# Longer planned times for loads and transposes, later first-layer weights, and four output buffers in a planned attention + mixer kernel

## Chip, cores and metric

One core of one Trainium2 chip. The metric is the device time of one execution in microseconds (us). The kernel before takes 647.9 us (median of three runs, 647.58 to 648.09).

## The reference

```python
# q, k, v: (8, 12, 448, 64) float32, tau = 0.1
q_n = q / (norm(q, axis=-1) + 1e-6);  k_n = k / (norm(k, axis=-1) + 1e-6)
attn = softmax(q_n @ k_n^T / tau)                  # per batch and head, 448 x 448
x = (attn @ v) as (8, 448, 768)
# mixer: U (448, 32), V (32, 448), w_ch1 (768, 3072), w_ch2 (3072, 768)
u = x + (x^T @ U @ V)^T
out = u + relu(u @ w_ch1) @ w_ch2
```

## The kernel before

The kernel has no fixed loop order. It first lists every operation with a planned duration, then a small planner runs the list against a model of the engines and sorts all operations by planned start. That order is what each engine's queue gets, and the trace shows the engine keep to it: in the changed kernel a ScalarE `ln` whose input was there at 59.9 us ran at 68.34, behind the `relu`s planned before it. A wrong planned duration therefore costs nothing in itself; it changes **which instruction stands behind which**. Planned times below come from running this planner by itself.

```python
class Plan:
    def run(self): ...          # greedy: an engine takes the first operation that is ready
                    if isinstance(o.lat, tuple):          # a transfer
                        q, work, fixed = o.lat
                        dma[q] = max(dma[q], o.end) + work      # its queue, one after the other
                        o.end = dma[q] + fixed                  # and a fixed time on top
                    else:
                        o.end += o.lat

def load(fn, busy, deps=(), acq=(), rel=()):              # issued by GpSimd
    return plan.add(Op("POOL", 0.8, fn, ..., lat=("in", busy, 2.0)), pool_q)

r_O = ring(2, [128, CH], FP, "O_sb")                      # results on their way out
r_mm = ring(3, [128, 512], FP, "mm", psum)                # PSUM banks for all but scores and attn @ v

# ... stats(b): VectorE squares and sums q and k per head, ScalarE takes ln and exp,
#     VectorE normalises; then xn is transposed (batches 0, 1: TensorE; others: DMA) ...
o = Op("ACT/DVE" if b == 0 else "DVE", dve_t(256 * (a1 - a0), 2), None, ...)      # the square

# ... stage0(b): U and V products (TensorE), u = x + h (VectorE), transposes of u ...

def mlp(b, us, uT, ut):
    for f in range(NC): ...                               # first layer: 24 x 6 matmuls into one mm bank each
    work = [(i, t, half) for i, t in enumerate(tiles) for half in range(2)]
    side = 3 if b == 0 else 1                             # batch 0: three results side by side,
    for w0 in range(0, len(work), side):                  # since w2 is still arriving
        mms = [Slot(r_mm, 1) for _ in range(side)]
        ...                                               # second layer: 24 matmuls per result
        o = plan.add(Op("DVE", ..., nc.vector.tensor_add(O.tile, mm.tile, us[i]), acq=[O], rel=[mm, us[i]]))
        plan.add(Op("SP", 0.1, nc.sync.dma_start(out=..., in_=O.tile...), rel=[O], prio=2, lat=2.5))

hold = load_v(0, 4, 12)                                   # the rest of v of batch 0
for i in range(NW):
    w1_ops.append(load_w1(i, NW, hold[-4:-3]))            # w1 after the fourth-last of these
```

Of the kernel before, what the change touches and what calls it, by code (L numbers as in the profile page):

```python
# [10 lines left out]
FP = mybir.dt.float32  # L11
# [187 lines left out]
def kernel(  # L199
# [25 lines left out]
    inv_tau = 1.0 / float(tau)  # L225
    EPS = 1e-6
    PE_BATCHES = 2

    const = ctx.enter_context(tc.tile_pool(name="const", bufs=1))
    pool = ctx.enter_context(tc.tile_pool(name="pool", bufs=1))  # L230
# [13 lines left out]
    def fixed_ring(tiles):  # L244
# [15 lines left out]
    r_u = ring(8, [128, C], BF, "u_nat")  # L260
    r_uT = ring(1, [128, CC, 512], BF, "uT")

    r_w2 = Ring(1, lambda i: pool.tile([128, H, 4, D], FP, name="v_raw", tag="w2", bufs=1)
                if i == 0 else pool.tile([128, NC, C], BF, name="w2_sb", tag="w2", bufs=1))
    w2, v_raw = Slot(r_w2, 1), Slot(r_w2, 6)
    r_relu = ring(1, [128, NC, 512], BF, "relu")
    r_O = ring(2, [128, CH], FP, "O_sb")
    r_rd = ring(2, [128, 4, 1], FP, "rd")
    r_mm = ring(3, [128, 512], FP, "mm", psum)
    r_sc = ring(3, [128, 512], FP, "sc", psum)  # L270
    r_av = ring(2, [128, 4, D + 8], FP, "av", psum)


    U_f = const.tile([128, 2, 4, R], FP, name="U_f")
    U_sb = const.tile([128, 2, 4, 128], BF, name="U_sb")
    V_f = const.tile([R, S], FP, name="V_f")
    V_sb = const.tile([128, PAD + S + PAD], BF, name="V_sb")
    ident = const.tile([128, 128], BF, name="ident")
    w1_sb = const.tile([128, CC, F], BF, name="w1_sb")
# [30 lines left out]
    def dve_t(n, fast=1):  # L310
        return 0.09 + n * 0.00104 / fast

    def load(fn, busy, deps=(), acq=(), rel=()):
        return plan.add(Op("POOL", 0.8, fn, deps=deps, acq=acq, rel=rel,
                           lat=("in", busy, 2.0)), pool_q)

    def fill(fn, n=256, prio=8, eng="DVE", deps=()):
        return plan.add(Op(eng, 0.1 + n * 0.0005, fn, deps=deps, prio=prio))


    def load_w1(i, n, deps):
# [33 lines left out]
    def load_qk(b, h0, h1):  # L355
        ld = Slot(r_ld, 3 * (h1 - h0) // 2)
        ops = [load(lambda i=i, src=src: nc.gpsimd.dma_start(  # L357
            out=ld.tile[:, i, 0:h1 - h0, :],
            in_=src[b, h0:h1].rearrange("h (s c) d -> s h (c d)", c=SC)),
            (h1 - h0) * 0.5, acq=[ld]) for i, src in enumerate((q, k))]  # L360
        return ld, ops

    def load_v(b, h0, h1):


        vb = v_t[b % 2]
        old = [v_set[b % 2]] + [last_av.get((b - 2, h // 2)) for h in range(h0, h1)]
        ops = []
        for hh in range(2):
            hs = slice(h0 + hh, h1, 2)  # L370
            for j in range(4):
                if j < 3:
                    lo, hi, base = 128 * j + 64 * hh, 128 * j + 64 * hh + 128, 0
                else:
                    lo, hi, base = (384, 448, 0) if hh == 0 else (0, 64, 64)
                for n, c, s0, s1 in segments(lo, hi):
                    p0 = base + n - lo
                    src = v[b, hs].rearrange("h (s c) d -> c s h d", c=SC)[c, s0:s1]
                    busy = (s1 - s0) * (h1 - h0) * 0.001
                    if b == 0:  # L380
                        ops.append(plan.add(Op("SP", 0.45, lambda j=j, s0=s0, s1=s1, p0=p0, hs=hs,
                                               src=src: nc.sync.dma_start(
                            out=v_raw.tile[p0:p0 + s1 - s0, hs, j, :], in_=src),
                            acq=[v_raw], lat=("x", busy, 2.0), prio=-2)))
                    else:
                        ops.append(load(lambda j=j, s0=s0, s1=s1, p0=p0, hs=hs, src=src:
                            nc.gpsimd.dma_start(out=vb[p0:p0 + s1 - s0, hs, j, 0:D], in_=src),  # L387
                            busy, deps=old))
        loads = ops
        if b == 0:  # L390
            def cast(p, hs, j):
                return plan.add(Op("POOL", 1.2 if j.stop == 3 else 0.3, lambda: nc.gpsimd.tensor_copy(  # L392
                    out=vb[p, hs, j, 0:D], in_=v_raw.tile[p, hs, j, :]),
                    deps=ops + old, rel=[v_raw]), pool_v)
            ops = [cast(slice(0, 128), slice(h0, h1), slice(0, 3)),
                   cast(slice(0, 64), slice(h0, h1, 2), slice(3, 4)),
                   cast(slice(64, 128), slice(h0 + 1, h1, 2), slice(3, 4))]
        for h in range(h0, h1):
            got[b, h, "v"] = ops
        return loads  # L400
# [43 lines left out]
    def norm(b, p, ld, inv, a, deps, pr):  # L444


        by_pe = b < PE_BATCHES
        xn, qkT = Slot(r_xn, 2 if by_pe else 1), Slot(r_qkT, 7)
        deps = deps + [xn_set[count[0] % len(xn_t)]]
        count[0] += 1  # L450

        def part(i, hh):
            def fn():
                src = ld.tile[:, i, a:a + 2, :].rearrange("p h (c d) -> p h c d", d=D)
                sc = inv.tile[:, i, a:a + 2, :].unsqueeze(3)
                if i == 0:
                    dst = xn.tile[:, 8:12, :].rearrange("p c (h d) -> p h c d", h=2)
                    nc.vector.tensor_mul(dst, src, sc.to_broadcast([SCH, 2, SC, D]))  # L458
                else:
                    dst = xn.tile[:, 4 * hh:4 * hh + 4, 64 * hh:64 * hh + 64]  # L460
                    nc.vector.tensor_mul(dst, src[:, hh], sc[:, hh].to_broadcast([SCH, SC, D]))  # L461
            return plan.add(Op("DVE", dve_t(512 if i == 0 else 256), fn, deps=deps, acq=[xn],
                               rel=[ld, inv] if (i, hh) != (1, 0) else [ld, inv], prio=pr))

        ops = [part(1, 0), part(1, 1), part(0, 0)]
        if not by_pe:
            done = [plan.add(Op("SP", 0.1, lambda: nc.sync.dma_start_transpose(
                out=qkT.tile, in_=xn.tile.rearrange("p b e -> p (b e)")), deps=ops, acq=[qkT],
                rel=[xn], prio=0, lat=("x", 0.05 * 84, 2.0)))]
        else:  # L470
            done = []
            for b0, b1 in ((0, 8), (8, 12)):
                done.append(flip(
                    pe_tp, [(lambda z=z: xn.tile[:, z, :]) for z in range(b0, b1)], SCH,
                    lambda: qkT.tile, (lambda t_, x, b0=b0, b1=b1: (t_[:, b0:b1, :], x)),
                    ops, [qkT], [xn]))
        got[b, p, "qkT"] = (qkT, done)
# [127 lines left out]
    def mlp(b, us, uT, ut):  # L605
# [25 lines left out]
        for w0 in range(0, len(work), side):  # L631
# [11 lines left out]
            for (i, t, half), mm in zip(work[w0:w0 + side], mms):  # L643
# [5 lines left out]
                for bb in (b - par, b - par + 1):  # L649
                    o0 = (bb % 2) * S  # L650
                    lo, hi = max(128 * t, o0), min(128 * (t + 1), o0 + S)
                    if lo >= hi:
                        continue
                    for nn, j, p0, p1 in segments(lo - o0, hi - o0):
                        r0 = nn + o0 - 128 * t
                        O.uses += 1
                        O.left += 1
                        plan.add(Op("SP", 0.1, lambda bb=bb, j=j, p0=p0, p1=p1, r0=r0, O=O, hs=hs:
                            nc.sync.dma_start(out=rows(out[bb], j, p0, p1)[:, hs],
                                              in_=O.tile[r0:r0 + p1 - p0, :]),  # L660
                            deps=[o], rel=[O], prio=2, lat=2.5))

    def copy_op(op, dst, src):
        if op.by == "ACT":
# [19 lines left out]
        nc.vector.memset(U_sb, 0.0)  # L684
        nc.vector.memset(V_sb, 0.0)

    zf = fill(lambda: nc.vector.memset(U_f, 0.0), 256, prio=-4)
    z = fill(zero, 1500, prio=-0.2)

    def load_u(par):  # L690
        off = PAD * par
        ops = []
        for t in range(4):
            lo, hi = max(0, 128 * t - off), min(S, 128 * (t + 1) - off)
            for n, c, s0, s1 in segments(lo, hi):
                r0 = n + off - 128 * t
                ops.append(plan.add(Op("SP", 0.45, lambda t=t, c=c, s0=s0, s1=s1, r0=r0: nc.sync.dma_start(
                    out=U_f[r0:r0 + s1 - s0, par, t, :], in_=rows(moe_U, c, s0, s1)),
                    deps=[zf], prio=-2, lat=2.5)))
        return ops  # L700

    def cast_u(par):
        nc.gpsimd.tensor_copy(out=U_sb[:, par, :, 0:R], in_=U_f[:, par])

    def cast_v():
        nc.gpsimd.tensor_copy(out=V_sb[0:R, PAD:PAD + S].rearrange("r (c s) -> r s c", c=SC),
                              in_=V_f.rearrange("r (s c) -> r s c", c=SC))


    w1_ops, w2_ops = [], []  # L710
# [13 lines left out]
        return stage0(b, X, muls)  # L724

    u0 = load_u(0)
    v0 = plan.add(Op("SP", 0.45, lambda: nc.sync.dma_start(out=V_f, in_=moe_V), prio=-2, lat=2.5))
    first = load_qk(0, 0, 2)
    id_set = plan.add(Op("POOL", 0.5, lambda: make_identity(nc, ident)), pool_q)
    stats(0, 0, 2, *first)  # L730
# [4 lines left out]
    hold = load_v(0, 4, 12)  # L735
    u1 = load_u(1)
    for i in range(NW):
        w1_ops.append(load_w1(i, NW, hold[-4:-3]))
    consts = [plan.add(Op("POOL", 0.5, lambda: cast_u(0), deps=u0 + [z]), pool_v),
              plan.add(Op("POOL", 1.5, cast_v, deps=[v0, z]), pool_v),  # L740
              plan.add(Op("POOL", 0.5, lambda: cast_u(1), deps=u1 + [z]), pool_v)]
    state[0] = att(0)
    go(1, 0, 4)
    go(1, 4, 8)
# [52 lines left out]
```

## Time and profile before

| | kernel before |
|---|---|
| span of the profiled run | 647.6 us |
| TensorE work at full rate (worked out in the prediction) | 578.6 us |
| lost: span less that work | 69.0 us |
| of it up to 72 us / 72 to 105 / 105 to 137 | 34.0 / 3.8 / 8.3 |
| 137 to 170 / 170 to 260 / behind 260 | 9.4 / 6.5 / 7.2 |
| VectorE busy from 120 to 220 us | 89.6 of 100 us |

"Lost" is the wall time of a stretch less the full-rate time of the matmuls in it: waits, and running at half clock. It is the measure used all through this text. Read it by stretch, since the busy share of TensorE (93%) mixes a start that is full of waits with 390 us that have almost none. The stretches here differ a little from those in the prediction. Where a trace lacks matmul records, the table's sum is up to 2 us too high, and a single line of it is good to about half a microsecond; span less 578.6 is then the right total.

### The profile page before, as it was taken

The page shows a single profiled execution, that of the slowest core. Times are in us where ns is not written, and L with a number is a line of the kernel's source. Part 1 is how long each engine was busy: PE and PEld are TensorE (multiplying, and loading weights), DVE is VectorE, ACT ScalarE, POOL GpSimd, SP SyncE. Part 2 cuts the span into 40 slices and gives each one's busy share as a digit, 9 for nine tenths or more (in the row PEclk, how much of TensorE's full clock was granted, in tenths as well). Part 3 has the DMA queues.
Part 4 walks back from the last instruction along what each step waited for, and adds up shares of the span by engine and source line. Part 5 has one row for each costly group of instructions (what it writes and reads, how often), then busy time and mean ns, then how long its engine had stood idle before and what let it go on. Part 6 is the DMA issues. An engine that isn't in the chain of part 4 may idle for free.

```text
span 647.6 us, 11512 instructions
## 1 busy us (share of the span) xinstructions
PE 603.9 (93%) x4682; PEld 354.6 (55%) x4682; DVE 303.5 (47%) x736; ACT 286.3 (44%) x605; POOL 114.3 (18%) x175
## 2 busy tenths in 40 slices
PE   2879999696999889999999999999999999999997
PEld 1455665363654457566644566566644666654464
DVE  7946978797999856852670124103410120010011
ACT  5853882485685108650864108640744004204400
POOL 3164533161343400700150000000000000000000
PEclk9987999799899999999999999999999999999999
DMA  9979998999699915924590314212000310210011
GB/s 128 172 134 160 180 204 64 157 131 169 62 159 133 174 45 87 182 30 88 99 134 0 59 53 82 30 25 74 15 13 0 74 50 12 62 55 7 0 50 49
DMA packets 150180, 55.09 MB, mean 85 GB/s; under 512 B 115280, under 2 KB 150128, under 8 KB 150128
## 3 DMA queue, kind: packets, MB, share of 16 engines
q0 software_dynamic: 67840, 25.27, 35.2%
q1 hardware_dynamic: 82288, 29.09, 24.3%
q8 instruction: 36, 0.59, 0.4%
q14 instruction: 16, 0.13, 0.1%
HBM read 52.08 MB, written 11.01 MB: 97 GB/s over the span
## 4 chain that ended last, share of the span: by engine, by line
PE 69%; DVE 14%; DMA 11%; SPq 1%; issue 1%; ACT 1%; POOL 1%; ACTq 0%; POOLq 0%; DVEq 0%
PE mm L637 28%; PE mm L614 27%; PE av L506 6%; PE sc L491 6%; DMA v_raw<-in_v_dram 4%; DVE ss L424 4%; DMA qkT<-xn 4%; DMA qk_nat<-in_k_dram 2%; DVE sq L420 2%; DVE xn L461 2%; DVE xn L458 2%; PE mm L562 1%; DMA qk_nat<-in_q_dram 1%; PE mm L534 1%; DVE X_sb L514 1%
## 5 line engine op out<-in xcount | busy, mean ns | idle before, releaser
L637 PE MATMUL mm<-w_sb,relu 128*128 128x384 bf16 x1344 | 237.0, 327 | 4.8 <-DVE O_sb L647 4.4
L614 PE MATMUL mm<-uT,w_sb 128*128 128x512 bf16 (+1 forms) x1152 | 233.6, 355 | 0.2 <-DVE u_nat L576 0.2
L495 ACT ACTIVATE attn<-sc 128x448 bf16<-128x448 f32 x336 | 159.5, 551 | 110.8 <-PE av L506 69.1
L637 PEld LDWEIGHTS <-relu 128*128 128x128 bf16 x1344 | 131.7, 98 | 100.3 <-issue 12.1
L614 PEld LDWEIGHTS <-w_sb 128*128 128x128 bf16 x1152 | 113.2, 99 | 106.6 <-issue 4.2
L624 ACT ACTIVATE relu<-mm 128x512 bf16<-128x512 f32 (+1 forms) x182 | 98.8, 545 | 157.7 <-PE mm L614 157.4
L647 DVE TENSOR_TENSOR O_sb<-mm,u_nat 128x384 f32<-128x384 f32 x56 | 30.9, 554 | 260.3 <-PE mm L637 248.6
L491 PE MATMUL sc<-qkT 128*128 128x448 bf16 x336 | 100.4, 369 | 6.8 <-ACT qkT L665 3.2
L506 PEld LDWEIGHTS <-attn 128*128 128x128 bf16 x1536 | 62.7, 100 | 25.0 <-issue 9.3
L506 PE MATMUL av<-v_nat,attn 128*128 128x65 bf16 x1536 | 66.8, 197 | 6.4 <-POOL v_nat L392 3.3
L387 POOL DMA_DIRECT2D v_nat<-in_v_dram x98 | 63.1, 650 | 37.4 <-DMA w_sb<-in_moe_w_ch_dram 9.8
L424 DVE TENSOR_REDUCE ss<-sq 112x8 f32<-112x512 bf16 x96 | 65.4, 683 | 2.8 <-ACT sq L418 0.3
L357 POOL DMA_DIRECT2D qk_nat<-in_q_dram x25 | 17.9, 714 | 157.1 <-DVE xn L458 145.1
L491 PEld LDWEIGHTS <-qkT 128*128 128x128 bf16 x336 | 30.0, 101 | 28.1 <-issue 7.0
L514 DVE TENSOR_TENSOR X_sb<-av,rd 128x256 bf16<-128x256 f32 x96 | 40.8, 425 | 3.3
L420 DVE TENSOR_TENSOR sq<-qk_nat 112x512 bf16<-112x512 bf16 x89 | 37.4, 421 | 3.7 <-DMA qk_nat<-in_q_dram 3.7
L461 DVE TENSOR_TENSOR xn<-qk_nat,inv 112x256 bf16<-112x256 bf16 x96 | 36.6, 419 | 3.2 <-DMA qkT<-xn 2.6
L512 DVE RECIPROCAL rd<-av 128x4 f32<-128x4 f32 x96 | 17.2, 179 | 38.5 <-PE av L506 38.4
L458 DVE TENSOR_TENSOR xn<-qk_nat,inv 112x512 bf16<-112x512 bf16 x48 | 32.9, 685 | 0.0
L576 DVE TENSOR_TENSOR u_nat<-mm,X_sb 128x384 bf16<-128x384 f32 (+2 forms) x48 | 24.8, 552 | 8.8 <-PE mm L562 8.5
L562 PE MATMUL mm<-A_sb,V_sb 128*128 128x384 bf16 (+2 forms) x64 | 17.8, 340 | 9.5 <-DVE O_sb L647 5.1
L429 ACT ACTIVATE ln<-ss 112x32 f32<-112x32 f32 (+1 forms) x25 | 5.8, 231 | 39.8 <-DVE ss L424 39.7
(41 smaller groups left out, 158.4 us busy)
## 6 DMA issues: line engine op xcount, KB each, us to landing
qk_nat<-in_q_dram POOLq DMA_DIRECT2D x23, 224.0 KB, 6.1
qk_nat<-in_k_dram POOLq DMA_DIRECT2D x23, 224.0 KB, 7.8
w_sb<-in_moe_w_ch_dram POOLq DMA_DIRECT2D x4, 1152.0 KB, 12.3
w_sb<-in_moe_w_ch_dram POOLq DMA_DIRECT2D x8, 576.0 KB, 13.9
out_dram<-O_sb SPq DMA_DIRECT2D x16, 168.0 KB, 2.2
out_dram<-O_sb SPq DMA_DIRECT2D x16, 144.0 KB, 2.1
out_dram<-O_sb SPq DMA_DIRECT2D x16, 120.0 KB, 2.0
out_dram<-O_sb SPq DMA_DIRECT2D x16, 96.0 KB, 2.2
```

The costliest lines, as they stand in the source:

```text
L387: nc.gpsimd.dma_start(out=vb[p0:p0 + s1 - s0, hs, j, 0:D], in_=src),
L420: nc.vector.tensor_mul(y, x, x)
L424: lambda i=i, a0=a0, a1=a1, sq=sq: nc.vector.reduce_sum(ss.tile[:, i, a0:a1, :].rearrange("p h c -> p (h c)"), sq.tile[:, 0:a1 - a0, :].re ...
L458: nc.vector.tensor_mul(dst, src, sc.to_broadcast([SCH, 2, SC, D]))
L461: nc.vector.tensor_mul(dst, src[:, hh], sc[:, hh].to_broadcast([SCH, SC, D]))
L491: nc.tensor.matmul(out=sc.tile[:, 0:S], lhsT=kT, rhs=qkT.tile[:, 8:12, :].rearrange("p c s -> p (c s)"), start=True, stop=True)
L495: exps[m] = plan.add(Op("ACT", act_t(S), lambda sc=sc, m=m: nc.scalar.activation(out=attn.tile[:, m, off:off + S], in_=sc.tile[:, 0:S], fu ...
L506: o = plan.add(Op("PE", 0.033, lambda t=t, j=j, h=h, hh=hh, av=av: nc.tensor.matmul(out=av.tile[:, t, 0:D + 1], lhsT=attn.tile[:, 3 if j = ...
L514: muls.append(plan.add(Op("DVE", dve_t(256), lambda av=av, rd=rd, h=h: nc.vector.tensor_mul(X.tile[:, :, h * D:(h + 1) * D], av.tile[:, :, ...
L614: o = plan.add(Op("PE", pe_t(n), lambda f=f, cc=cc, mm=mm: nc.tensor.matmul(out=mm.tile[:, 0:n], lhsT=w1_sb[:, cc, f * 128:(f + 1) * 128], ...
L624: nc.scalar.activation(out=relu.tile[:, f, 0:n], in_=mm.tile[:, 0:n], func=AF.Relu)
L637: nc.tensor.matmul(out=mm.tile[:, 0:CH], lhsT=relu.tile[:, f, i * 128:(i + 1) * 128], rhs=w2.tile[:, f, half * CH:(half + 1) * CH], start= ...
```

## The change

The intent: (1) ask for w1 only when the whole first v is in, so that 1152 KB weight pieces do not stand beside v's last transfers; (2) plan loads of q, k and v from batch 1 on, and the DMA transposes, with 8 us in place of 2, since they take 6 to 8 us in the trace; (3) four output buffers in place of two, their stores planned at 4.0 us. U and V's raw copies move into the buffer of v's to make room. By the planner it changes the planned order of the first 30 us and of nothing later.

```diff
+    LATE = 8.0
-    r_O = ring(2, [128, CH], FP, "O_sb")
+    r_O = ring(4, [128, CH], FP, "O_sb")
 (load(): a parameter late=2.0 takes the place of the fixed 2.0)
-            (h1 - h0) * 0.5, acq=[ld]) for i, src in enumerate((q, k))]
+            (h1 - h0) * 0.5, acq=[ld], late=2.0 if b == 0 else LATE) for i, src in enumerate((q, k))]
 (load_v, batches from 1 on)
-                            busy, deps=old))
+                            busy, deps=old, late=LATE))
 (DMA transposes of xn)
-                rel=[xn], prio=0, lat=("x", 0.05 * 84, 2.0)))]
+                rel=[xn], prio=0, lat=("x", 0.05 * 84, LATE)))]
 (output stores)
-                            deps=[o], rel=[O], prio=2, lat=2.5))
+                            deps=[o], rel=[O], prio=2, lat=4.0))
-        w1_ops.append(load_w1(i, NW, hold[-4:-3]))
+        w1_ops.append(load_w1(i, NW, hold[-1:]))
 (cut: v_raw, U_f and V_f become views of one tile "raw"; its users acquire and release it)
```

More of the change, by code (lines that the diff above doesn't have):

```diff
@@ L261, with v_raw, U_f, V_f @@
     r_uT = ring(1, [128, CC, 512], BF, "uT")
-    r_w2 = Ring(1, lambda i: pool.tile([128, H, 4, D], FP, name="v_raw", tag="w2", bufs=1)
+    r_w2 = Ring(1, lambda i: pool.tile([128, H * 4 * D + 8 * R + S], FP, name="raw", tag="w2", bufs=1)
                 if i == 0 else pool.tile([128, NC, C], BF, name="w2_sb", tag="w2", bufs=1))
-    w2, v_raw = Slot(r_w2, 1), Slot(r_w2, 6)
+    w2, raw = Slot(r_w2, 1), Slot(r_w2, 9)
+    def v_raw():
+        return raw.tile[:, 0:H * 4 * D].rearrange("p (h j d) -> p h j d", h=H, j=4)
+    def U_f():
+        return raw.tile[:, H * 4 * D:H * 4 * D + 8 * R].rearrange("p (b t r) -> p b t r", b=2, t=4)
+    def V_f():
+        return raw.tile[0:R, H * 4 * D + 8 * R:H * 4 * D + 8 * R + S]
     r_relu = ring(1, [128, NC, 512], BF, "relu")
-    r_O = ring(2, [128, CH], FP, "O_sb")
+    r_O = ring(4, [128, CH], FP, "O_sb")
     r_rd = ring(2, [128, 4, 1], FP, "rd")
@@ L271 @@
     r_av = ring(2, [128, 4, D + 8], FP, "av", psum)
-    U_f = const.tile([128, 2, 4, R], FP, name="U_f")
     U_sb = const.tile([128, 2, 4, 128], BF, name="U_sb")
-    V_f = const.tile([R, S], FP, name="V_f")
     V_sb = const.tile([128, PAD + S + PAD], BF, name="V_sb")
@@ L311, in dve_t, with load, fill @@
         return 0.09 + n * 0.00104 / fast
-    def load(fn, busy, deps=(), acq=(), rel=()):
+    def load(fn, busy, deps=(), acq=(), rel=(), late=2.0):
         return plan.add(Op("POOL", 0.8, fn, deps=deps, acq=acq, rel=rel,
-                           lat=("in", busy, 2.0)), pool_q)
-    def fill(fn, n=256, prio=8, eng="DVE", deps=()):
-        return plan.add(Op(eng, 0.1 + n * 0.0005, fn, deps=deps, prio=prio))
+                           lat=("in", busy, late)), pool_q)
+    def fill(fn, n=256, prio=8, acq=()):
+        return plan.add(Op("DVE", 0.1 + n * 0.0005, fn, acq=acq, prio=prio))
     def load_w1(i, n, deps):
@@ L382, in load_v @@
                                                src=src: nc.sync.dma_start(
-                            out=v_raw.tile[p0:p0 + s1 - s0, hs, j, :], in_=src),
-                            acq=[v_raw], lat=("x", busy, 2.0), prio=-2)))
+                            out=v_raw()[p0:p0 + s1 - s0, hs, j, :], in_=src),
+                            acq=[raw], lat=("x", busy, 2.0), prio=-2)))
                     else:
@@ L392, in cast @@
                 return plan.add(Op("POOL", 1.2 if j.stop == 3 else 0.3, lambda: nc.gpsimd.tensor_copy(
-                    out=vb[p, hs, j, 0:D], in_=v_raw.tile[p, hs, j, :]),
-                    deps=ops + old, rel=[v_raw]), pool_v)
+                    out=vb[p, hs, j, 0:D], in_=v_raw()[p, hs, j, :]),
+                    deps=ops + old, rel=[raw]), pool_v)
             ops = [cast(slice(0, 128), slice(h0, h1), slice(0, 3)),
@@ L685, in zero @@
         nc.vector.memset(V_sb, 0.0)
-    zf = fill(lambda: nc.vector.memset(U_f, 0.0), 256, prio=-4)
+    zf = fill(lambda: nc.vector.memset(U_f(), 0.0), 256, prio=-4, acq=[raw])
     z = fill(zero, 1500, prio=-0.2)
@@ L697, in load_u @@
                 ops.append(plan.add(Op("SP", 0.45, lambda t=t, c=c, s0=s0, s1=s1, r0=r0: nc.sync.dma_start(
-                    out=U_f[r0:r0 + s1 - s0, par, t, :], in_=rows(moe_U, c, s0, s1)),
+                    out=U_f()[r0:r0 + s1 - s0, par, t, :], in_=rows(moe_U, c, s0, s1)),
                     deps=[zf], prio=-2, lat=2.5)))
@@ L702, in cast_u @@
     def cast_u(par):
-        nc.gpsimd.tensor_copy(out=U_sb[:, par, :, 0:R], in_=U_f[:, par])
+        nc.gpsimd.tensor_copy(out=U_sb[:, par, :, 0:R], in_=U_f()[:, par])
     def cast_v():
         nc.gpsimd.tensor_copy(out=V_sb[0:R, PAD:PAD + S].rearrange("r (c s) -> r s c", c=SC),
-                              in_=V_f.rearrange("r (s c) -> r s c", c=SC))
+                              in_=V_f().rearrange("r (s c) -> r s c", c=SC))
     w1_ops, w2_ops = [], []
@@ L726 @@
     u0 = load_u(0)
-    v0 = plan.add(Op("SP", 0.45, lambda: nc.sync.dma_start(out=V_f, in_=moe_V), prio=-2, lat=2.5))
+    v0 = plan.add(Op("SP", 0.45, lambda: nc.sync.dma_start(out=V_f(), in_=moe_V), acq=[raw], prio=-2, lat=2.5))
     first = load_qk(0, 0, 2)
@@ L737 @@
     for i in range(NW):
-        w1_ops.append(load_w1(i, NW, hold[-4:-3]))
-    consts = [plan.add(Op("POOL", 0.5, lambda: cast_u(0), deps=u0 + [z]), pool_v),
-              plan.add(Op("POOL", 1.5, cast_v, deps=[v0, z]), pool_v),
-              plan.add(Op("POOL", 0.5, lambda: cast_u(1), deps=u1 + [z]), pool_v)]
+        w1_ops.append(load_w1(i, NW, hold[-1:]))
+    consts = [plan.add(Op("POOL", 0.5, lambda: cast_u(0), deps=u0 + [z], rel=[raw]), pool_v),
+              plan.add(Op("POOL", 1.5, cast_v, deps=[v0, z], rel=[raw]), pool_v),
+              plan.add(Op("POOL", 0.5, lambda: cast_u(1), deps=u1 + [z], rel=[raw]), pool_v)]
     state[0] = att(0)
```

## The prediction

> **What bounds the kernel now.** I read the page first (busy shares, then the 40 slices).
>
> ```profile
> PE 603.9 (93%) x4682; PEld 354.6 (55%) x4682; DVE 303.5 (47%) x736; ACT 286.3 (44%) x605; POOL 114.3 (18%) x175
> ...
> PE   2879999696999889999999999999999999999997
> ...
> DVE  7946978797999856852670124103410120010011
> ...
> PEclk9987999799899999999999999999999999999999
> DMA  9979998999699915924590314212000310210011
> ```
>
> TensorE is the bound, and from slice 16 on (about 260 us) it is full. What can be saved lies before that, where TensorE has holes and DMA is nearly full too. To size it I went to the chain of work that ended last, in order of time.
>
> ```profile
> 20.88 14.10 DMA v_raw<-in_v_dram
> ...
> 118.12 4.04 DMA out_dram<-O_sb
> ...
> 153.09 7.40 DMA qk_nat<-in_k_dram
> ...
> 557.64 23.40 PE mm L637 x144
> 581.04 31.08 PE mm L614 x144
> ```
>
> The last two lines give the full rate: 23.40/144 = 162.5 ns for a matmul of 384 columns and 31.08/144 = 215.8 ns for 512, which is N/2.4 + 2.5 ns. The same view has 32 `av` matmuls in 1.01 us (31.6 ns each) and 3 scores in 0.57 us (190 ns each). With the counts of the groups by form: 1344 x 162.5 + 576 x 215.8 + 576 x 162.5 (the two MLP layers: 436.3) + 336 x 189 (scores: 63.6) + 1536 x 31.6 (`av`: 48.5) + transposes and the small low-rank matmuls (30.2) = 578.6 us. The span is 647.6, so 69 us are lost: waiting, or running under full rate. I added up the difference between wall time and full-rate time of the matmuls stretch by stretch: 9.0 us before the first matmul; 22.0 from there to the first MLP matmul at 51.7; 2.3 from 51.7 to 60; 4.6 from 60 to 105; 8.3 from 105 to 129; 9.4 from 129 to 168; 6.4 from 168 to 240; 2.8 from 240 to the last matmul; 4.5 behind it. The time-ordered list of TensorE says what the large ones are:
>
> ```profile
> 31.36 0.35 PE L491 MATMUL sc<-qkT 128*128 128x448 bf16 x1
> 34.36 1.01 PE L506 MATMUL av<-v_nat,attn 128*128 128x65 bf16 x19 [2.65 <-POOL v_nat L392]
> ...
> 118.04 0.50 PE L637 MATMUL mm<-w_sb,relu 128*128 128x384 bf16 x2
> 122.89 0.80 PE L637 MATMUL mm<-w_sb,relu 128*128 128x384 bf16 x2 [4.36 <-DVE O_sb L647]
> 123.49 1.32 PE L491 MATMUL sc<-qkT 128*128 128x448 bf16 x3
> ...
> 160.48 0.48 PE L562 MATMUL mm<-A_sb,V_sb 128*128 128x384 bf16 x1 [3.34 <-DMA qk_nat<-in_k_dram]
> ...
> 225.14 0.32 PE L562 MATMUL mm<-A_sb,V_sb 128*128 128x384 bf16 x1 [2.74 <-DVE O_sb L647]
> ```
>
> Three scores span 1.32 us behind the 4.36 us wait, against 0.73 elsewhere: each long hole is followed by some us at half clock. And VectorE at the same two moments:
>
> ```profile
> 122.28 0.56 DVE L647 TENSOR_TENSOR O_sb<-mm,u_nat 128x384 f32<-128x384 f32 x1 [1.58 <-DMA out_dram<-O_sb]
> ...
> 159.87 0.56 DVE L647 TENSOR_TENSOR O_sb<-mm,u_nat 128x384 f32<-128x384 f32 x1 [3.21 <-DMA out_dram<-O_sb]
> ```
>
> So the wait at 160 that the tool puts down to a qk load is really an output store: the third of a group of three results found both output buffers still being stored, VectorE stood still on it, the PSUM bank under it stayed taken, and TensorE stopped.
>
> [...]
>
> ```profile
> qk_nat<-in_q_dram POOLq DMA_DIRECT2D x23, 224.0 KB, 6.1
> qk_nat<-in_k_dram POOLq DMA_DIRECT2D x23, 224.0 KB, 7.8
> ...
> qkT<-xn SPq DMA_TRANSPOSE x36, 5.9
> ```
>
> [...]the v transfers that SyncE issues from 16.2 to 18.8 us land in 2.0 to 2.7 us; the four issued from 19.3 on, after GpSimd asked for two w1 pieces of 1152 KB at 18.5 and 19.3, take 8.5 to 14.1. [...]0.5 is granted from 121.3 to 128.1 and from 158.9 to 165.7.
>
> **The change, part by part.** The instruction counts stay the same (the same number of TensorE rows in both orders), so 578.6 us of full-rate work stay; only the loss can move.
>
> *First weight after the whole v.* In the new GpSimd order all casts of v, then those of U and V, stand before the first w1 transfer. Without w1 beside them the last v transfers (issued by 20.9) should land as their neighbours do, by about 23.3 instead of 35.0. That removes the 2.65 us wait and most of the half-clock stretch behind it (36.0 to 39.4 in the clock record, about 1.3 lost); ScalarE, idle 3.9 us there, is the next limit. I take 4.5 of the 22.0. The price: w1 is issued near 28 instead of 18.5 and 38. In the trace the second pair of pieces landed 9.0 and 14.4 us after 38.05 with nothing in front of it, 5.4 us per piece, so four land near 37, 42, 48 and 53. The first MLP matmul moves to about 47, and a piece feeds 36 matmuls = 5.9 us, so they are needed at 47, 53, 59 and 65. Hidden. DMA work up to w2 is the same sum, so w2's last piece still lands near 91 (91.9 before).
>
> *Longer planned loads and transposes from batch 1.* No cost on any engine; it moves the planned order. In the new TensorE order 132 of the 144 first-layer matmuls of batch 0 run before batch 1's first transposes (59 before); batch 1's attention then interleaves with w2 matmuls instead. Piece by piece: those 132 end near 70, batch 1's q and k have landed by 61, and the 72 w2 matmuls of the first group come sparsely (34 of them among 128 `av` and some 25 scores, then 38 in a row near 86 to 93) while w2 pieces land from 72 to 92, 2.8 apart. That just fits; I leave 4.0 of the 4.6 lost there. Farther on, VectorE work that reads a fresh load stands later in its queue, so that the O_sb and u_nat adds that free PSUM no longer stand behind it: the 2.7 us wait at 225, one of 1.8 at 235 and the 1.1 us ones. I take 4.4 of 6.4 and 0.8 of 2.8.
>
> *Four output buffers.* The third O_sb of a group no longer waits for a store (5 us landing then). That removes the holes of 4.4 and 3.3 us and the half clock behind them, 2.6 us and 2.0 us. In the new VectorE order the three adds of a group stand together. I take 7.5 of 8.3, and 6.9 of 9.4.
>
> Sum: 4.5 + 0.6 + 7.5 + 6.9 + 4.4 + 0.8 = 24.7 us. Nothing is taken from the start, the tail (same order at the end) or the 2.3 at half clock at the first MLP matmul. 69.3 - 24.7 = 44.6 lost; 578.6 + 44.6 = **623 us**.
>
> **Rivals.** (a) *The weights become the wait.* DMA is 90% busy up to 90 us; if w1 moves more slowly beside the U loads, or w2 lands at 95 or more, TensorE stands at the start of MLP 0 or inside the first w2 group, and falls to half clock. For it: w2's fit is within a microsecond. Against: totals are unchanged, and the U loads are small. It would cost 3 to 8 us: 626 to 631. (b) *Another in-order block takes the place.* The plan's times for loads are now above the 6 to 8 us of the trace, but a busier VectorE (14 of 15 us in several stretches before 210) can still fall behind its plan, and the stall moves to another PSUM bank. If only the two output-buffer holes go (11 us with half clock) and v (4.5): 632. (c) *v was hidden.* ScalarE and VectorE were 88% busy from 15 to 30 us, so an earlier v could just run into them; then 2 instead of 4.5 us: 625. (d) *The plan holds better than I allow*: the losses between 60 and 260 nearly vanish: 615.
>
> **Range and chances.** The buffer holes are certain to go, I think, and with their half-clock time they are 11 of the 13 us that 2% asks for (634.9); v or the order need give only 2 more. 80% range **614 to 635**; faster by over 2%: 0.86; within: 0.13; slower: 0.01.
>
> **What would show it.** Right: v's last landing before 25 us and no GpSimd wait of 12.7 us on it; no wait of VectorE on output stores before 240 us; no half clock between 60 and 240; the first w1 matmul near 47; w1 and w2 waits of TensorE under 2 us together. Wrong: TensorE waiting for a w_sb transfer, for xn or qkT around 70, or for a PSUM bank freed by VectorE late in stretches 105 to 240; or a first MLP matmul still at 51.

## More of the kernel before

Line numbers: the changed kernel has 9 lines more, so L637 of before (second layer) is L646 after, L614 is L623 (first layer), L506 is L515 (`av`), L534 and L562 of the U and V products are L543 and L571.

## The result, and the profile after

The changed kernel takes **639.8 us** (638.75 to 640.8, four runs) where the kernel before took 647.74 beside it: ratio 0.9882, 95% interval 0.9856 to 0.9908. That is 1.2% faster, within the 2% that the prediction gave a chance of 0.13, and outside its range of 614 to 635. Ratios, here and below, are the mean time of one kernel's fast runs over that of the other's fast runs of the same rounds, so not quite the ratio of the medians quoted.

From the page of the kernel after (same rows as in the prediction: busy TensorE, then slices of 16 us, in tenths):

```profile
PE 601.0 (94%) x4657; PEld 352.5 (55%) x4682; DVE 305.4 (48%) x742; ACT 283.7 (44%) x599; POOL 115.1 (18%) x175
...
PE   3789989979999999999999999999999999999997
...
DVE  8963674999999989664480134104400220010011
```

The slices of VectorE are the thing to see. Before they read 7946978797999856852; now they start 8963674 and then read 9 in eight slices of nine: VectorE has more air from 48 to 112 us and less from 112 to 256. By stretch, as lost us:

| stretch, us | before | after | change | predicted |
|---|---|---|---|---|
| 0 to 72 | 34.0 | 28.9 | -5.2 | -4.5 (v), and part of -0.6 |
| 72 to 105 | 3.8 | 7.8 | **+4.0** | the rest of -0.6 |
| 105 to 137 | 8.3 | 9.0 | **+0.7** | -7.5 (buffers) |
| 137 to 170 | 9.4 | 3.5 | -5.9 | -6.9 (buffers) |
| 170 to 260 | 6.5 | 7.2 | **+0.7** | -4.4 (order) |
| behind 260 | 7.2 | 5.9 | -1.3 | -0.8 |
| span less 578.6 | 69.0 | 60.3 | -8.7 | -24.7 |

Three of the six lines came about as said. The rest is in the time-ordered list of TensorE after (start, us, line, tile, count, and in brackets the idle time before it and what ended it):

```profile
48.69 3.62 PE L623 MATMUL mm<-uT,w_sb 128*128 128x384 bf16 x12
...
88.11 1.23 PE L515 MATMUL av<-v_nat,attn 128*128 128x65 bf16 x32 [2.12 <-DVE X_sb L523]
...
116.82 10.56 PE L646 MATMUL mm<-w_sb,relu 128*128 128x384 bf16 x64
129.51 0.60 PE L543 MATMUL mm<-X_sb,U_sb 128*128 128x256 bf16 x4 [2.13 <-DVE O_sb L656]
...
132.26 0.39 PE L571 MATMUL mm<-A_sb,V_sb 128*128 128x256 bf16 x1 [0.89 <-DVE u_nat L582]
```

The first MLP matmul stands at 48.69 (51.67 before) and the 60th at 59.8 (64.2). The hole at 118 to 123 is gone: 64 second-layer matmuls run through it without a wait. But behind them, at 127 to 135, stands the second part of batch 1's chain (U and V products, `u` additions and transposes; the part for columns 512 to 767) with nothing else left to run; the first part ran at 106 to 113. Before the change the whole chain ran at 89 to 103, among first-layer matmuls:

```profile
97.83 0.60 PE L534 MATMUL mm<-X_sb,U_sb 128*128 128x256 bf16 x4
98.27 0.98 PE L614 MATMUL mm<-uT,w_sb 128*128 128x384 bf16 x5
```

And VectorE at two earlier moments:

```profile
55.55 0.43 DVE L429 TENSOR_TENSOR sq<-qk_nat 112x512 bf16<-112x512 bf16 x1 [6.06 <-DMA qk_nat<-in_q_dram]
...
60.22 0.69 DVE L433 TENSOR_REDUCE ss<-sq 112x8 f32<-112x512 bf16 x1
68.85 0.18 DVE L444 TENSOR_SCALAR ln<-ln 112x32 f32<-112x32 f32 x1 [7.95 <-ACT ln L441]
...
98.59 0.42 DVE L523 TENSOR_TENSOR X_sb<-av,rd 128x256 bf16<-128x256 f32 x1
104.22 1.49 DVE L656 TENSOR_TENSOR O_sb<-mm,u_nat 128x384 f32<-128x384 f32 x3 [5.21 <-PE mm L646]
```

VectorE has the four sums of batch 1's first four heads at 59.9 (the fifth sum shown is of the next ones), and from 60.9 on it stands still for 8 us. What it waits for is a 0.22 us `ln` on ScalarE:

```profile
67.95 0.49 ACT L633 ACTIVATE relu<-mm 128x384 bf16<-128x384 f32 x1 [0.48 <-PE mm L623]
68.34 0.22 ACT L438 ACTIVATE ln<-ss 112x32 f32<-112x32 f32 x1
```

The sums are there, and ScalarE is half idle (busy for 4.90 of the 9.75 us from 58.20 to 67.95), but its queue is worked off in order here: the `ln` stands behind a row of `relu`s that come one per 0.98 us, and runs at 68.34, after the last of them. It stands there because the plan has batch 1's loads land at 58.4 to 68.4 us, and they land at 55.5 to 61.5. For batch 2 the plan says 104.8 to 114.8 and they land at 94.1 to 100.05; that is the second idle stretch, 99.0 to 104.2, with data in hand: batch 2's first square runs at 112.3. The plan already counts 2.0 us of queue per load (the trace: 1.2 between landings) and now adds 8 on top of the queue. From batch 3 on the longer time is about right: the landings of q and k come between 0.3 us before and 6.7 us behind the plan, where the old plan was 13 to 25 us early from the end of batch 3 to batch 5. That lateness is not the transfers' own. In the kernel before the q load of batch 4's middle four heads, say, is asked for at 152.4 where the plan has 136.0, and takes 5.1 us where the plan has 6.3; the whole run has fallen behind its plan there, and the 8 us make up for that.

No wait of TensorE for a weight is in the trace (w1 lands at 36.5, 43.0, 48.6 and 55.0; the prediction's estimate was 37, 42, 48 and 53), and none of VectorE for an output store before 240 us.

### The profile page after: what moved, and what is told of

Same layout as the page of the kernel before. It is cut to its first block, busy times and chain, and to the rows that moved or that the text cites. A ratio compares the mean times of both kernels' runs of the same rounds, so it can differ in the third digit from the quotient of the medians.

```text
span 638.9 us, 11472 instructions
## 1 busy us (share of the span) xinstructions
PE 601.0 (94%) x4657; PEld 352.5 (55%) x4682; DVE 305.4 (48%) x742; ACT 283.7 (44%) x599; POOL 115.1 (18%) x175
## 4 chain that ended last, share of the span: by engine, by line
PE 69%; DVE 25%; ACT 2%; DMA 1%; issue 1%; SPq 1%; POOL 0%; ACTq 0%; DVEq 0%
PE mm L623 29%; PE mm L646 29%; DVE ss L433 6%; PE sc L500 4%; PE av L515 4%; DVE sq L429 3%; DVE X_sb L523 3%; DVE xn L470 3%; DVE xn L467 3%; DVE u_nat L585 1%; ACT attn L504 1%; PE mm L543 1%; DMA raw<-in_v_dram 1%; PE mm L571 1%; DVE relu L635 1%
## 5 line engine op out<-in xcount | busy, mean ns | idle before, releaser
L623 PE MATMUL mm<-uT,w_sb 128*128 128x384 bf16 (+1 forms) x1129 | 232.4, 354 | 1.2 <-ACT relu L633 0.2
L646 PE MATMUL mm<-w_sb,relu 128*128 128x384 bf16 x1344 | 232.3, 327 | 0.2 <-ACT qkT L674 0.2
L623 PEld LDWEIGHTS <-w_sb 128*128 128x128 bf16 x1152 | 112.8, 98 | 105.9 <-issue 7.0
L633 ACT ACTIVATE relu<-mm 128x384 bf16<-128x384 f32 (+1 forms) x179 | 97.0, 542 | 160.0 <-PE mm L623 159.6
L500 PE MATMUL sc<-qkT 128*128 128x448 bf16 x336 | 98.2, 364 | 5.5 <-ACT attn L504 2.3
L515 PEld LDWEIGHTS <-attn 128*128 128x128 bf16 x1536 | 61.5, 99 | 23.6 <-issue 4.7
L470 DVE TENSOR_TENSOR xn<-qk_nat,inv 112x256 bf16<-112x256 bf16 x96 | 36.5, 418 | 0.5
L352 PE MATMUL tp<-ident,xn 112*128 112x112 bf16 x144 | 11.2, 227 | 11.6 <-DVE xn L470 8.9
```

The costliest lines, as they stand in the source:

```text
L470: nc.vector.tensor_mul(dst, src[:, hh], sc[:, hh].to_broadcast([SCH, SC, D]))
L500: nc.tensor.matmul(out=sc.tile[:, 0:S], lhsT=kT, rhs=qkT.tile[:, 8:12, :].rearrange("p c s -> p (c s)"), start=True, stop=True)
L515: o = plan.add(Op("PE", 0.033, lambda t=t, j=j, h=h, hh=hh, av=av: nc.tensor.matmul(out=av.tile[:, t, 0:D + 1], lhsT=attn.tile[:, 3 if j = ...
L623: o = plan.add(Op("PE", pe_t(n), lambda f=f, cc=cc, mm=mm: nc.tensor.matmul(out=mm.tile[:, 0:n], lhsT=w1_sb[:, cc, f * 128:(f + 1) * 128], ...
L633: nc.scalar.activation(out=relu.tile[:, f, 0:n], in_=mm.tile[:, 0:n], func=AF.Relu)
L646: nc.tensor.matmul(out=mm.tile[:, 0:CH], lhsT=relu.tile[:, f, i * 128:(i + 1) * 128], rhs=w2.tile[:, f, half * CH:(half + 1) * CH], start= ...
```

## The experiments

Four calls, each on one chip with its own runs of the kernel before. Times below are medians of four runs unless said.

### Taking one part away at a time

**late_from_b3**: loads of batches 1 and 2 planned at 2 us as before, 8 us from batch 3 on; transposes stay at 8.

```diff
-  late=2.0 if b == 0 else LATE     (q, k)          +  late=2.0 if b < 3 else LATE
-  late=LATE                        (v)             +  late=2.0 if b < 3 else LATE
```

> The changed kernel, but the q, k and v loads of batches 1 and 2 are planned with the old 2 us instead of 8; loads from batch 3 on and the transposes keep 8. Theory A (in the changed kernel the plan puts the landing of batch 1 and 2 loads 3 to 15 us later than they land, because the queue in front of them is already in the plan, so VectorE work stands late in its queue and VectorE idles 8 us around 61 to 69, then is behind): the wait of VectorE on ACT ln of 7.9 us goes, the time falls to 627 to 635. Theory B (VectorE is simply full between 69 and 135 us, whatever the order): 638 to 641, as the changed kernel.

Measured 636.5 us, ratio 0.9833 [0.9801, 0.9865]. The 7.8 us lost at 72 to 105 fell to 2.2, as the reading of the `ln` says. But the chain of batch 1 moved to 105 to 117 and lost 10.7 us in the stretch of 105 to 137, so only 3 us reached the end. The time lies between theory A's range and theory B's.

**no_late**: all loads and transposes at 2 us; late w1 and four buffers stay (`LATE = 2.0`).

> The changed kernel with all loads and transposes planned at the old 2 us (w1 after v and four output buffers kept). Theory A: the early loss of about 5 us comes back, but VectorE runs ahead of its loads again from batch 3 on, which costs about as much: 635 to 641. The account in the prediction (the longer times are worth 5 us): 644 to 646. If the longer times do only harm: under 633.

Measured 645.8 us, ratio 0.9982 [0.9925, 1.0039]. Two of the three parts together, without the third, are worth nothing that is clear of noise; theory A's 635 to 641 missed, the prediction's account of the longer times was right beside the other parts. 16.0 us are lost at 170 to 260, more than in any other run; but the run that was profiled is the slowest of the four (651.0 us), so read its losses as high by some microseconds. In the list of waits of this kernel (us in total, times, longest):

```profile
DVE sq L429 <- DMA qk_nat<-in_q_dram: 16.0, 5, 7.7
```

**two_bufs**: two output buffers planned at 2.5 us, the rest of the change stays.

> The changed kernel with two output buffers and the old planned store time. The account in the prediction (the holes of 4.4 and 3.3 us and their half clock, 11 us): 649 to 652. Rival (the adds into the output buffer come late because VectorE is late, so the buffers matter less): 639 to 644.

Measured 641.95 us, ratio 0.9914 [0.9879, 0.995]. Beside the other parts, four buffers are worth some 2 us (the intervals overlap), not 14.4. With two, the planner sets another order. VectorE still stands on a store twice, for 2.60 us until 106.7 and for 3.04 us until 223.1, more than in the kernel before; but TensorE has other work then (1.0 us lost at 104 to 107, 5.00 of 5.00 us busy at 219 to 224). The same chain loses 8.4 us at 105 to 126.

**w1_old**: w1 asked for early again (`hold[-4:-3]`), the rest stays.

> The changed kernel with the first w1 transfer asked for where it was (before the second part of v). If the move gives what the first stage shows (first MLP matmul 51.7 to 48.7 us): 642 to 644. Rival (the later weights push everything behind them and cost more than v gains): 634 to 638. If it is neither: 639 to 641.

Measured 643.8 us, ratio 0.9941 [0.9904, 0.9978]: beside the other parts, the w1 step is worth 4 us. Its mechanism is plain in this kernel's list of TensorE; v is waited for again:

```profile
32.78 1.22 PE L515 MATMUL av<-v_nat,attn 128*128 128x65 bf16 x16 [5.45 <-POOL v_nat L401]
```

### One part alone

**only_late** (early w1, two buffers), **only_bufs** (early w1, 2 us), **only_w1** (two buffers, 2 us): the changed kernel with the other two parts put back (the move of the raw copies stays).

> The kernel before with the longer planned times alone (8 us for loads and transposes from batch 1 on); w1 is asked for early as before and there are two output buffers planned at 2.5 us. If the parts add up as they did when taken away one at a time from the changed kernel (w1 4 us, buffers 2 us), 645 to 647. If they overlap, since without the longer times the other two were worth 1 us together, the longer times alone keep their 6 us: 640 to 643. The prediction had 5 us for them alone: 643.

> The kernel before with four output buffers (store planned at 4.0 us) alone. The prediction gave them 14.4 us, from the two holes of 4.4 and 3.3 us and the half clock behind each: 633 to 636. Theory R (each hole hides another wait of nearly the same length right behind it, as the chip run without longer times suggests, which with the weights' part won 1 us in all): 645 to 648, no wait of VectorE on an output store, but 7 to 10 us lost in the same stretch, 105 to 130 us, on batch 1's U and V chain or on fresh loads.

> The kernel before with the first weight asked for once v is in, alone (two output buffers planned at 2.5 us, loads and transposes at 2 us). The prediction gave this part 4.5 + 0.6 us: 642 to 643. Theory V (the parts do not add, since each sets another planned order in which VectorE becomes the bound): with four buffers this part had cost 4.5 us (641.6 for the buffers alone, 645.8 for both), with longer times and two buffers it had won 13; alone I expect the start to win 2 to 4 us and the order behind it to take most of it back: 644 to 648.

Measured 655.2, 641.6 and 650.9 us. All eight combinations, as ratios to the kernel before beside them:

| | 2 us, early w1 | 2 us, late w1 | 8 us, early w1 | 8 us, late w1 |
|---|---|---|---|---|
| two buffers | 1 | 1.0057 | **1.0123** | 0.9914 |
| four buffers | **0.9913** | 0.9982 | 0.9941 | 0.9882 |

(Widest interval: 0.0057 to either side.) Longer times alone make the kernel 8 us slower; late w1 alone makes it 4 us slower; four buffers alone give 5.6 us. The three effects sum to +0.9%, and together they measure -1.2%. **No part has a price of its own here**: each sets a new order for all five engines. My expectation for only_late missed on both of its branches, only_bufs fell between its two, and only_w1 came out above even the pessimistic one.

only_bufs is the cleanest test of the prediction's largest term, since its planned order from 30 to 105 us is that of before. The store waits go. In its list of TensorE the 4.36 us hole has become 1.46 us, at full clock:

```profile
118.81 0.79 PE L646 MATMUL mm<-w_sb,relu 128*128 128x384 bf16 x2 [1.46 <-DVE O_sb L656]
```

Of the 4.36 us only 1.58 were the store's. The kernel before has other work of VectorE between the second and the third addition of the group; with four buffers the three additions stand together:

```profile
117.14 1.01 DVE L647 TENSOR_TENSOR O_sb<-mm,u_nat 128x384 f32<-128x384 f32 x2
118.08 0.42 DVE L461 TENSOR_TENSOR xn<-qk_nat,inv 112x256 bf16<-112x256 bf16 x1
...
120.28 0.42 DVE L420 TENSOR_TENSOR sq<-qk_nat 112x512 bf16<-112x512 bf16 x1
```

The loss falls by 4.7 us at 105 to 137 (8.3 to 3.6) and by 4.9 at 137 to 170 (9.4 to 4.5), then rises by 2.3 at 170 to 260. So on the old order the buffers are worth 9.6 where they act and lose a quarter of it later. VectorE, free of the store waits, is now busy for 96.4 of the 100 us from 120 to 220.

**late_b12**: 8 us for the loads of batches 1 and 2 alone; everything else at 2 us.

> The changed kernel with 8 us planned for the loads of batches 1 and 2 alone; the loads from batch 3 on and the transposes are planned at 2 us as before. Theory V (longer times for batches 1 and 2 say their data is later than it is, TensorE and VectorE stand idle at 72 to 105, and VectorE, busy without a break from 120 to 260, never makes it up; from batch 3 on the longer times are right and win): with no longer times 645.8 was measured, so 647 to 652 here, the 7 us lost at 72 to 93 stay, and 10 or more are lost at 170 to 260. Rival (it is the number of batches that matters, longer times win wherever they are): 640 to 645.

Measured 644.6 us, ratio 0.9957 [0.9935, 0.998]. The stretches came as theory V said (6.4 us lost at 72 to 105, 13.0 at 170 to 260), the total did not: against no_late, what is lost early (+3.9) is won back at 105 to 170 (-5.4). So planning batches 1 and 2 too late costs TensorE where it happens, but is no net loss in that order; the theory was wrong there, and the rival's 640 to 645 was right. (The profiled run of no_late is a slow one, as said, so differences of these stretches are rough.) What the longer times win beside the other parts, they win mostly from batch 3 on: late_from_b3 is 9 us faster than no_late, late_b12 1 us. The longer time of the transposes goes with late_from_b3 and was not tested apart.

### Is it banks, or VectorE?

With the second group of three results holding all three `mm` banks, batch 1's chain cannot start before that group ends. **after_split** does the second three one by one:

```diff
-        side = 3 if b == 0 else 1
-        for w0 in range(0, len(work), side):
+        sides = [3, 1, 1, 1] if b == 0 else [1] * len(work)
+        for w0, side in zip([sum(sides[:i]) for i in range(len(sides))], sides):
```

> The changed kernel with one edit: the six second-layer products of batch 0, which share the three mm banks of PSUM in two groups of three, are done as one group of three and then three single ones (one bank each). Theory F (filler used up): batch 1's short chain of U and V products, additions and transposes cannot start while the second group of three holds all the mm banks, and stands bare behind it (7.0 us lost at 126 to 137 us in the changed kernel). Then single products leave banks for it: of the 7.0 us 3 to 5 go, the loss in 105 to 140 falls from 9.5 to 4 to 6 us and the time from 639.8 to 634 to 637. Rival G (the chain is bound by VectorE and ScalarE themselves, or by late results): no change, 638.5 to 641, and the loss only moves.

Measured 639.7 us, ratio 0.9879 [0.9846, 0.9912]: nothing. The loss moved from 126 to 137 (7.0 to 0.6) to 105 to 126 (2.0 to 7.2). In the changed kernel batch 1's attention itself ends at 117, so the chain's second part has no results to start from before that, banks or not. Theory F fell for this kernel.

**late3_split**: the same edit on late_from_b3, where attention ends at 98 and the chain starts at 105.9, behind the first group of three.

> Both edits together: the loads of batches 1 and 2 planned at 2 us as before (8 from batch 3 on), and batch 0's second-layer products as one group of three and three single ones. With the loads' edit alone 636.5 us were measured, with 10.2 us lost at 105 to 126 us behind the second group of three. Theory F (filler held back by the three banks): 4 to 7 of the 10.2 go, 630 to 633 us, and the first MLP matmul of batch 1 starts at 126 to 128 instead of 132. Rival G (the chain is bound by VectorE and ScalarE, not by banks): 635 to 638, the first MLP matmul of batch 1 still behind 130.

Measured 632.05 us (631.12 to 633.88), ratio 0.9768 [0.9737, 0.9799]. Here the banks were the limit, the other way round: the chain holds back the second group of three, whose first three matmuls start one by one (115.24, 116.05, 117.34) as the chain gives a bank back. TensorE in late_from_b3, then in late3_split:

```profile
114.50 0.90 PE L352 MATMUL tp<-ident,u_nat 128*128 128x128 bf16 x13 [0.37 <-DVE u_nat L585]
115.24 0.33 PE L646 MATMUL mm<-w_sb,relu 128*128 128x384 bf16 x1
116.05 0.32 PE L646 MATMUL mm<-w_sb,relu 128*128 128x384 bf16 x1 [0.49 <-ACT uT L674]
117.34 14.36 PE L646 MATMUL mm<-w_sb,relu 128*128 128x384 bf16 x70 [0.97 <-ACT uT L674]
132.03 1.24 PE L623 MATMUL mm<-uT,w_sb 128*128 128x512 bf16 x5 [0.32 <-DVE O_sb L656]
```

```profile
113.75 1.95 PE L646 MATMUL mm<-w_sb,relu 128*128 128x384 bf16 x11
115.54 1.06 PE L352 MATMUL tp<-ident,u_nat 128*128 128x128 bf16 x16
116.43 10.08 PE L646 MATMUL mm<-w_sb,relu 128*128 128x384 bf16 x61
126.34 1.03 PE L623 MATMUL mm<-uT,w_sb 128*128 128x512 bf16 x3
```

Up to 113 us the chain is the same in both, 1 us later in late3_split. Then second-layer matmuls fill its last 4 us, and with that gap the half clock behind it goes (granted from 116.3 to 123.1 in late_from_b3: 70 matmuls in 14.36 us, 205 ns each; 61 in 10.08 us, 165 ns, in late3_split). Batch 1's first layer starts at 126.3 instead of 132.0, and the loss at 105 to 137 is 5.0 instead of 10.7.

Next, VectorE. **after_sq** and **late3_split_sq** let the planner give the squares of q and k to ScalarE in every batch when VectorE is busy:

```diff
-                o = Op("ACT/DVE" if b == 0 else "DVE", dve_t(256 * (a1 - a0), 2), None,
+                o = Op("ACT/DVE", dve_t(256 * (a1 - a0), 2), None,
```

> The changed kernel with one edit: the planner may give the squares of q and k to ScalarE in every batch, when VectorE is busy, not in batch 0 alone. Theory V (VectorE is the bound from 120 to 260 us in the changed kernel: 95% busy in 120 to 220): VectorE's work in 120 to 260 falls by 6 to 12 us, the loss of 10.7 us at 137 to 260 falls by 3 to 6, time 634 to 637. Rival R (TensorE's waits there come of the order in which loads land, not of VectorE's amount of work): 638 to 642.

> The fastest kernel so far (632.05 us: loads of batches 1 and 2 planned at 2 us, batch 0's second layer as one group of three and three single products) with the same edit: squares of q and k on ScalarE or VectorE in every batch. There 11.2 us are lost at 137 to 260 with VectorE 95% busy. Theory V: 4 to 7 of these go: 625 to 628. Rival R: 630 to 634.

Measured 636.1 us (ratio 0.9831 [0.9811, 0.9852]) and **626.0 us** (625.63 to 627.02, ratio 0.9677 [0.9658, 0.9696]). Both lie in theory V's range. The loss at 137 to 260 fell from 10.7 to 6.5 and from 11.2 to 6.0. late3_split_sq is the fastest correct kernel: 3.2% under the kernel before, and 13.8 us under the changed one by the medians. It was run at another time.

This edit changes the order too. So **after_thin** takes work off VectorE and leaves every order as it is (the planner gives the same list with and without the edit): from batch 1 on a square covers one head of two, and the sum reads it twice (relative error 0.38; the instructions are as many as before). Its output is wrong, which doesn't matter for the time.

```diff
+                        if b > 0:
+                            x, y = x[:, 0:1, :], y[:, 0:1, :]
                         nc.vector.tensor_mul(y, x, x)
 (and reduce_sum reads sq.tile[:, 0:1] broadcast to both heads)
```

> The changed kernel, wrong on purpose: from batch 1 on VectorE squares only one of each two heads and sums that one twice, so a square takes about 0.25 instead of 0.41 us. The plan, and with it every engine's order, stays as it is. Some 44 squares stand at 137 to 260 us, about 7 us less VectorE work there, and nothing else changes. Theory V (VectorE's amount of work is the bound from 120 to 260): of the 10.7 us lost at 137 to 260, 3 to 6 go, 634 to 637. Rival R (moving squares to ScalarE had won by the new order alone): 638.5 to 641.

> The kernel before with the same wrong-on-purpose edit, order unchanged. VectorE is busy 89.5 of the 100 us from 120 to 220 there (97 in the changed kernel) and waits for output stores and for TensorE. Theory V (the bound moved to VectorE only with the change): 0 to 3 us won, 644.5 to 647.5. Rival (VectorE was the bound here already): 4 to 7 won, 640 to 643.

> The changed kernel without the longer times (645.8 us), with the same wrong-on-purpose edit, order unchanged. 16.0 us are lost there at 170 to 260, and VectorE waits 16.0 us in all for fresh q loads, in order. If the waits for loads make that loss, less work on VectorE wins little: 643 to 647. If VectorE's amount of work makes it: 638 to 641.

Measured 631.75 (0.976 [0.9717, 0.9803]), 643.7 (0.9944 [0.9906, 0.9981]) and 639.8 us (0.9876 [0.9828, 0.9924]). The groups of VectorE at 137 to 260, in the changed kernel and in after_thin (busy us, mean ns, idle before):

```profile
L429 DVE TENSOR_TENSOR sq<-qk_nat 112x512 bf16<-112x512 bf16 x44 | 18.0, 409 | 0.0
```

```profile
L431 DVE TENSOR_TENSOR sq<-qk_nat 112x256 bf16<-112x256 bf16 x46 | 12.8, 277 | 0.0
```

A square takes 277 in place of 409 ns (the 0.25 us expected was an estimate). The 84 squares from batch 1 on (12 per batch) make 11.1 us less work, an estimate from these two rows, and **8 us of it reach the end**, below the 634 to 637 expected: between the two profiled runs about 5 us are won at 137 to 260, as theory V said, and 4 more at 72 to 137. VectorE, idle for half of the whole run, passes on more than two thirds of the work taken from it (8 of 11.1 us). On the kernel before the same edit gives 3.5 us (1.2 to 6.1 by the interval), somewhat more than the 0 to 3 I allowed: VectorE was already part of the bound there. On no_late it gives 6 us although its VectorE waits 16 us for loads; there it is both. The busy us of VectorE from 120 to 220 in before, after, after_thin and late3_split_sq (columns: wall, then busy us and instructions of TensorE, its weight loads, VectorE, ScalarE, GpSimd; granted clock; DMA; GB/s):

```profile
120.00:220.00 100.00, 90.30 (x762) 51.59 (x762) 89.56 (x219) 60.66 (x136) 40.95 (x62) 0.93 1.19 137
```

```profile
120.00:220.00 100.00, 91.82 (x776) 51.73 (x788) 96.80 (x237) 58.91 (x135) 35.05 (x53) 0.97 1.08 134
```

```profile
120.00:220.00 100.00, 94.88 (x807) 54.65 (x819) 96.07 (x246) 59.58 (x139) 39.04 (x60) 0.98 1.23 143
```

```profile
120.00:220.00 100.00, 97.42 (x832) 55.94 (x830) 90.03 (x215) 70.27 (x159) 39.62 (x60) 1.00 1.31 146
```

In after_thin VectorE is as busy as in the changed kernel: the time it saves it fills with the next work (246 instructions in place of 237), which is how a bound engine looks. In late3_split_sq ScalarE takes over 11 us of it and TensorE is busy for 97.4 of 100.

## Why the prediction was wrong

It said 623.0 us; 639.8 were measured. The work at full rate, 578.6 us, held. Of the gain of 24.7 us, 8.7 came. Two steps failed ("No cost on any engine" and the 5.2 us from the order), and one was mis-sized (the buffers).

- **"First weight after the whole v": right in the profile.** v's last transfer lands at 22.5 (said: by 23.3), the loss up to 72 us falls by 5.2 (said: 4.5 and some of 0.6), and weights are not waited for, so rival (a) is out. But only_w1 shows that a gain at the start is kept only if the order behind it lets it: alone the step makes the kernel 4 us slower.
- **"Four output buffers ... I take 7.5 of 8.3, and 6.9 of 9.4": the mechanism was right in part, the sum was mis-sized.** On the old order (only_bufs) it is 4.7 and 4.9 where the holes were, then 2.3 given back. The prediction's own lines gave less than it took: its items sum to 12.3 (holes of 4.4 and 3.3, half clock of 2.6 and 2.0), not 14.4, and VectorE's two waits for a store are 1.58 and 3.21 us, not the 4.36 and 3.34 of TensorE's holes. VectorE did not stand still on the store for the whole first hole; it worked until 120.7, and 1.5 us of that hole stay. In the whole change the term is 5.9 at 137 to 170 and nothing at 105 to 137, where the new order puts batch 1's chain behind the second-layer group; the sign that it listed, "a PSUM bank freed by VectorE late", is the 2.13 us wait at 129.5. I counted the same hole as won without asking what would stand there in the new order. "The buffer holes are certain to go, I think, and with their half-clock time they are 11 of the 13 us" is the sentence that made the chance of 0.86.
- **"Longer planned loads ... No cost on any engine": failed at 72 to 105.** The 8 us were set from the 6 to 8 us between issue and landing. That time has the queue in it (batch 1's loads land 1.2 us apart), and the plan counts the queue already: 2.0 us per load and 2.0 on top, so 4.0 behind the issue of a lone load. I saw that 132 first-layer matmuls now run before batch 1's transposes and took it for good, "that just fits". It left an `ln` behind `relu`s (input there at 59.9 us, run at 68.34), VectorE idle for 8 and 5 us with data in hand, and no first-layer work to put beside batch 1's chain. late_from_b3 shows the cost at that place: 7.8 us lost become 2.2. That no net loss came of it in every order (late_b12) is as said above.
- **"VectorE work that reads a fresh load stands later in its queue ... I take 4.4 of 6.4": failed.** There was next to nothing to win: from 60 to 260 us VectorE of the kernel before waits for q and k loads 0.8 us in all (0 after the change), so waits for fresh loads did not make its additions late. And VectorE has no time to give from 120 to 220: 96.8 of 100 us busy. after_thin shows this with the order held still. (No_late does wait 16.0 us for loads, but that is another order.) I had the figure, "14 of 15 us in several stretches before 210", wrote it under rival (b), and did not put it against my own term.
- **Rival (b), "another in-order block takes the place", 632,** was the nearest, and its reason held; it still counted both holes as won.

What stays open: what the move of the raw copies does by itself, and why early w1 with longer times alone is as slow as 655 us. Its losses are spread (13.4 us at 170 to 260, 11.8 at 105 to 137, 5.4 at 52 to 72, v waited for 9.0 us once), and I have no run that separates them.

## What to carry to other kernels

Where a planner sets the order, a planned time is not a safety margin: too long and a ready instruction stands behind unready ones (the `ln` here, for which VectorE waited 8 us), too short and a queue blocks on a load (16.0 us of VectorE in no_late); correct it against measured landings batch by batch. Before adding up holes to be won, look for the engine that will be full once they are gone: VectorE was 48% busy overall and 97% busy in the stretch that mattered, and the cheapest way to see whether it binds is to thin its work with the order unchanged. Test parts of a change in all combinations when they share a scheduler; single differences had even the wrong sign here.

## What the traces show of the clock, of loads and of squares

- In the changed kernel half clock is granted three times between start and end (44.9 to 51.7, 89.3 to 92.7, 130.2 to 137.1: 0.50, 0.50 and 0.51 in these stretches) without a long hole of TensorE before it: the longest single waits in the 4 us ahead were 0.93, 2.12 and 2.13 us, and TensorE was busy for 2.46, 1.88 and 1.87 of the 4.00 us. In the two long holes of the kernel before, the clock fell when TensorE had waited for 2.8 and 1.7 us (from 118.5 and 157.1 on, to 121.3 and 158.9). The length of a wait and the busy share do not settle it alone: in the kernel before TensorE was busy for only 1.26 of the 4.00 us from 221.2 to 225.2, with a wait of 2.74 us in them, and full clock (1.00) was granted there and up to 230. What settles it was not shown.

- A load of four heads reads 448 KB of float32 and writes the 224 KB that the profile lists. Medians from issue to landing are 6.1 and 7.8 us before, 5.3 and 6.6 after (below), and the queue is in them. What a planner needs beside them is the interval between landings in a full queue: 1.2 us per load in the changed kernel's batch 1.

```profile
qk_nat<-in_q_dram POOLq DMA_DIRECT2D x23, 224.0 KB, 5.3
qk_nat<-in_k_dram POOLq DMA_DIRECT2D x23, 224.0 KB, 6.6
```

- The squares of 512 and 256 columns took 409 and 277 ns (changed kernel and after_thin, 137 to 260 us). By their difference 145 ns of each do not go with the columns, an estimate that takes the rest as proportional to them. Halving a square saved a third of it.
